# Padding written early, one wide product of U and x, wide idle products and a longer allowance for GpSimd in a scheduled recurrence with a two-layer MLP

## The chip, the cores and the metric

One NeuronCore of a Trainium2 chip runs the whole program. The time is that of one execution in microseconds (us), as the device reports it; lower is better. Five engines work side by side, each through its own instructions in order: PE multiplies matrices (its weight loads are listed as PEld), DVE, ACT and POOL (GpSimd) do elementwise work, SP issues transfers, and ACT issues a few.

## The reference

For each of 4 batches and 8 heads a recurrence runs over 768 steps with a state of 48x48, and its output, 768 rows of 384 numbers for each batch, goes through a mixing term of rank 32 over the sequence and a two-layer MLP:

```python
for t in range(S):
    cur = einsum('bhd,bhe->bhde', u * k[t], v[t])
    y[t] = einsum('bhd,bhde->bhe', r[t], state + cur)
    state = w[:, None] * state + einsum('bhd,bhe->bhde', k[t], v[t])
x = y                                    # (4, 768, 384)
h = x.transpose(0, 2, 1) @ U @ V         # U: 768x32, V: 32x768
u_ = x + h.transpose(0, 2, 1)
out = u_ + relu(u_ @ w_ch1) @ w_ch2      # 384 -> 1536 -> 384
```

The inputs r, k, v, w and u are 32-bit floats. U, V and the two weight matrices are 64-bit floats.

## The kernel before

**Tiling.** A batch is cut into 6 chunks of 128 rows. Within a chunk the recurrence is written as products: scores of r with k (`pab`, L751), which a mask turns into `am` (L885), the scores times v (`pav`, L787), the carried state times r (`pav`, L793), and the new state from the scaled k and v (`pab`, L766; then `S`, L913, and its decayed copy `SW`, L922 or L926). r and k come in row by row and are turned on PE (`ptr`, `ptk`, L712); the turned copies are scaled into `rT` and `kT` by DVE or ACT. The scaled k itself is `ks` (L662): 8 heads of 48 numbers, each padded to 64 with zeros that a GpSimd memset writes (L661). There are two `ks` buffers. The diagonal term is `dv` (L669, L671, L681). The result of chunk n is `x` (L892).

The work of chunk n stands on PE in two halves, called first(n) and second(n) here: each does half of the outputs of chunk n and half of the scores of chunk n + 1. second(n) begins only after one small copy named `seen` (L866) of the first half's result.

**Order.** No loop runs on the chip. Python records every step as an operation with its engine, an estimate of its duration, what it reads and writes, and a key that gives its rank. `Plan.schedule` then plays the operations through its own estimates and fixes the order on each engine; where an operation may run on several engines (`on_either`, `one_of`), the estimates choose one. So a changed estimate may move instructions anywhere. Engines still wait for data by semaphores. Where the plan expects PE to idle, `plan.wakes` puts in products of the identity with itself that nobody reads (`wake`); it does so from the first product until the last product of U and x of batch 0, and in a second stretch behind it.

**Front.** Batch 0 has nothing to run beside. Its six chunks of attention come first (about 11 to 49 us). Each chunk's x is multiplied with U into the bank `wk` (`c_gx`, shown as `wake<-x,Uf`), the sum becomes `Gs` (L947, L948), and products of `Gs` and V finish the turned input of the MLP (`pu`, split into `uTh` and `uTl`). Meanwhile the 64-bit weights arrive and are made into floats, split in two parts: per block of 128x384 a pick of the high byte (L518 on DVE or L522 on ACT), a scale on ACT (L534), two integer operations on DVE (L525, L528), a rounded copy on ACT (L548) and a difference (L549, DVE or POOL). U and V go the same way (`raw_u`, `raw_v`).

**Rest.** From the first `p` product on, PE works through the MLP of batch 0 with the attention of batch 1 put in between, and so on through the batches. Each unit of the MLP is 9 products of 128x384 for the first layer and 9 for the second; the next attention fills the gaps.

Of the kernel before, what the change touches and what calls it, by code (L numbers as in the profile page):

```python
# [46 lines left out]
class Plan:  # L47
# [98 lines left out]
    def schedule(self):  # L146
        free = dict.fromkeys(self.AFTER, 0.0)
        cands = {e: [] for e in free}
        waiting, blocked = {}, []
        lock, queues, tiled, flying = 0.0, 0.0, False, {}  # L150
        for o in self.ops:
            o.behind -= o.deps
            waiting[o] = len(o.deps) + len(o.behind)
            o.out = []
        for o in self.ops:
            for p in o.deps | o.behind:
                p.out.append(o)

        def admit(o):
            for b in o.allocs:  # L160
                ring = self.rings[b.tag]
                k = sum(1 for x in o.allocs[:o.allocs.index(b)] if x.tag == b.tag)
                if ring["next"] + k >= len(ring["order"]) or ring["order"][ring["next"] + k] is not b:
                    return False
                if sum(f is not None for f in ring["free"]) <= k:
                    return False
            o.early, o.ends = max((p.start for p in o.behind), default=0.0), [(p.end, p.eng) for p in o.deps]
            for b in o.allocs:
                ring = self.rings[b.tag]
                i = min((i for i, f in enumerate(ring["free"]) if f is not None), key=lambda i: ring["free"][i][0])  # L170
                o.ends.append(ring["free"][i])
                if ring["last"] is not None:
                    o.early = max(o.early, ring["last"].start)
                ring["free"][i] = None
                ring["next"] += 1
                ring["last"] = o
                b.slot = i
            for i, way in enumerate(o.ways):
                cands[way[0]].append((o, i, self.ready_on(o, way[0])))
            return True  # L180

        def offer(os):
            blocked.extend(os)
            again = True
            while again:
                again = False
                for o in sorted(blocked, key=lambda o: o.key):

                    if all(self.rings[b.tag]["last"] is None or self.rings[b.tag]["last"].end is not None
                           for b in o.allocs) and admit(o):  # L190
                        blocked.remove(o)
                        again = True
        for o in self.ops:
            o.end = None
        offer([o for o in self.ops if not waiting[o]])
        left = len(self.ops)
        while left:
            best = None
            for e, cs in cands.items():
                if not cs:  # L200
                    continue
                at = []
                for o, i, ready in cs:
                    t = max(ready, free[e])
                    if o.ways[i][3]:
                        t = max(t, lock - (130 if e == "DVE" else 0))
                    at.append((t, o, i))
                now = min(t for t, _, _ in at)
                for t, o, i in sorted((a for a in at if a[0] <= now + 1), key=lambda a: a[1].key):
                    done = t + o.ways[i][1]  # L210
                    if e == "DVE" and len(o.ways) > 1:
                        done += self.BACKLOG * sum(q.ways[k][1] - self.OVERLAP[e] for u, q, k in at if u <= t and q.key > o.key)
                    if any(j != i and self.queue(o, w, cands[w[0]], free[w[0]], lock) < done - 1
                           for j, w in enumerate(o.ways)):
                        continue
                    if best is None or t < best[0]:
                        best = (t, o, i)
                    break
            t, o, i = best
            e, ns, fn, lk = o.ways[i]  # L220
            for w in o.ways:
                cands[w[0]] = [c for c in cands[w[0]] if c[0] is not o]
            if e == "PE":
                for begin, end, filler in self.wakes:
                    if begin.end is None or end.end is not None:
                        continue

                    x = free[e]
                    while self.pe_end(x, begin.ways[0][1], 0, False) < t - 150:
                        self.woken.append((x, filler))  # L230
                        x = self.pe_end(x, begin.ways[0][1], 0.8)
                        tiled = False
                    t = max(t, x)
                if o.tiled != tiled:
                    t, tiled = t + self.MODE, o.tiled
                ns = self.pe_end(t, ns, 0.65 if tiled else 0.85) - t
            o.start, o.eng, o.fn = t, e, fn
            free[e] = t + ns - self.OVERLAP[e]
            o.end = t + ns
            if lk:  # L240
                lock = o.end
            if o.dma:
                ring = flying.setdefault(e, [])
                room = self.RING - o.rows
                issued = t + ns
                for end, rows in reversed(ring):
                    room -= rows
                    if room < 0:
                        issued = max(issued, end)
                        break  # L250
                free[e] = issued + self.ISSUE[e]
                queues = max(queues, issued if issued == t + ns else t + ns) + o.dma
                ring.append((queues, o.rows))
                o.end, o.eng = queues + self.LANDS + o.late, "DMA"
            left -= 1
            new = []
            for p in o.out:
                waiting[p] -= 1
                if not waiting[p]:
                    new.append(p)  # L260
            for b in o.bufs:
                b.left -= 1
                if not b.left and b.tag:
                    end = max((u[0].end + (self.DRAINS if u[0].eng == "PE" else 0), u[0].eng) for u in b.uses)
                    self.rings[b.tag]["free"][b.slot] = end
            offer(new)
        return max(o.end for o in self.ops)
# [8 lines left out]
def dve(n):  # L276
    return 130 + 1.09 * n
# [6 lines left out]
def pool(n):  # L284
    return 180 + 2.15 * n
# [3 lines left out]
def rwkv_moe(ctx: ExitStack, tc: tile.TileContext, r, k, v, w, u, U, V, w1, w2, out):  # L289
    nc = tc.nc  # L290
    B, H, S, D = r.shape
    C = 128
    NCH = S // C
# [47 lines left out]
    def whole(*args, **kw):  # L341

        opened.clear()
        return nc.tensor.matmul(*args, **kw)  # L344

    def pe(ns, fn, w_, r_, tiled=False, dk=0.0):
        return op("PE", ns, fn, w_, r_, tiled=tiled, dk=dk)
# [6 lines left out]

    def on_either(n, fn, w_, r_, dk=0.0, only=None):

        ways = [("POOL", pool(n), lambda: fn(nc.gpsimd), True), ("DVE", dve(n), lambda: fn(nc.vector), True)]
        return one_of(ways, w_, r_, only, dk)

    def one_of(ways, w_, r_, only=None, dk=0.0):  # L360
# [38 lines left out]
    wk = bank("mm", "wake")  # L399
    awake = []  # L400

    def waking(bank_):

        def fn():
            whole(bank_.t[:, :128], lhsT=ident_, rhs=ident_, start=bank_ not in awake, stop=True, skip_group_check=True)
            awake.append(bank_)
        return fn

# [248 lines left out]
    def a_ks(n):  # L657

        kt, kb = ks_[n]
        ks = kss[n] = wbuf([128, H, HP], F32, "ks", NK, f"ks_{n}")  # L660
        op("POOL", 250, lambda: nc.gpsimd.memset(ks.t[:, :, D:], 0.0), [(ks, "pad")], [])  # L661
        on_either(384, lambda e: e.tensor_mul(ks.t[:, :, :D], kt()[:, :, :D], by_head(tab.t)), [(ks, "d")], kb + [tab],  # L662
                  only="DVE" if front(n) else None)

# [269 lines left out]

    def c_gx(n):

        for i in range(3):
            o = pe(225, lambda i=i: whole(wk.t[:3 * R, 128 * (i + 1):128 * (i + 2)], lhsT=Uf.t[:, n].rearrange("p k r -> p (k r)"),
                                      rhs=xs[n].t[:, 128 * i:128 * (i + 1)], start=False, stop=n == NCH - 1,
                                      skip_group_check=True), [(wk, "g")], [Uf, xs[n]])  # L940
        return o

    def c_g0():
        def pt():
# [359 lines left out]
    for t, _, f in sorted(steps, key=lambda s: s[:2]):  # L1304
        plan.key = t
        f()
    plan.wakes = [(*ends, gx[-1], fill), (*again, refill)]
    with tc.manual_schedule(engines={mybir.EngineType.PE, mybir.EngineType.SP, mybir.EngineType.DVE,
                                     mybir.EngineType.Activation, mybir.EngineType.Pool}):
        plan.run()  # L1310
# [34 lines left out]
```

## Time and profile before

| what | value |
|---|---|
| median of 3 runs | 438.04 us (437.14 to 439.49) |
| the profiled execution | 439.95 us, span 437.9 us |
| PE busy | 419.4 us (96%) |
| DVE busy | 267.8 us (61%) |
| ACT busy | 142.9 us (33%) |
| POOL busy | 55.6 us (13%) |
| mean granted clock of PE | 0.984 |

The span is what the profile covers; 2.05 us of the profiled execution's own time lie outside it. A granted clock of 1.00 is 2.4 GHz, one of 0.50 is 1.2 GHz. A busy share over the whole span says little here, since the front has other limits than the rest.

### The profile page before, as it was taken

To read this page: it belongs to the slowest core of one execution; us is meant where nothing else is said; L and a number is where in the kernel's file an instruction comes from. 1 tells how busy PE (TensorE), PEld (TensorE's weight loads), DVE (VectorE), ACT (ScalarE), POOL (GpSimd) and SP (SyncE) were. 2 spreads that over 40 slices of the span, in tenths; PEclk is the share of its full clock that TensorE was granted. 3 is DMA by queue.
4 is the path that set the end of the run, shared out by engine and by line. 5 is a ranking of instruction groups with operands and counts; after the bars stand their busy time and mean duration, and the time that the engine had idled before them with its cause. 6 is when DMAs were issued, how large, how long until landed. Compare 5 with 4: busy or idle time off the path is not lost.

```text
span 437.9 us, 12193 instructions
## 1 busy us (share of the span) xinstructions
PE 419.4 (96%) x5125; PEld 399.8 (91%) x5125; DVE 267.8 (61%) x602; ACT 142.9 (33%) x399; POOL 55.6 (13%) x92
## 2 busy tenths in 40 slices
PE   8889999999999999999999999999999999999991
PEld 8678899889999999999999999999999999999991
DVE  6979699999887757767775456567522351122121
ACT  1679679934421213121112221222112131111110
POOL 2651151223110002011100001101100000000000
PEclk9989699999999999999999999999999999999998
DMA  9979999654466876744586653231100510001001
GB/s 145 162 162 340 335 199 222 103 84 83 81 88 139 148 146 117 136 87 76 105 168 102 96 147 56 48 64 30 55 2 1 98 65 1 0 0 55 1 0 61
DMA packets 178975, 43.93 MB, mean 100 GB/s; under 512 B 168993, under 2 KB 175650, under 8 KB 178914
## 3 DMA queue, kind: packets, MB, share of 16 engines
q1 hardware_dynamic: 174162, 42.20, 46.9%
q10 hardware_dynamic: 4752, 0.89, 1.5%
q8 instruction: 42, 0.69, 0.7%
q14 instruction: 19, 0.16, 0.1%
HBM read 36.57 MB, written 6.49 MB: 98 GB/s over the span
## 4 chain that ended last, share of the span: by engine, by line
PE 81%; DVE 8%; ACT 3%; DMA 3%; POOL 1%; issue 1%; SPq 0%; ACTq 0%; DVEq 0%; POOLq 0%
PE p L344 64%; PE pav L787 5%; PE pav L793 4%; PE pu L344 3%; DVE raw_w L528 2%; DVE raw_w L525 2%; PE pab L751 2%; DMA ld<-in_r_dram 1%; DMA ld<-in_v_dram 1%; PE pab L766 1%; PE wake L344 1%; DVE hl L1081 1%; PE pG L958 1%; ACT dv L681 1%; POOL dv L671 1%
## 5 line engine op out<-in xcount | busy, mean ns | idle before, releaser
L344 PE MATMUL p<-uTh,w1s 128*128 128x384 f32 x576 | 148.2, 338 | 0.0
L1081 DVE SCALAR_TENSOR_TENSOR hl<-p,hh 128x384 fp32r<-128x384 f32 x96 | 53.2, 554 | 119.3 <-ACT hh L1080 119.0
L344 PE MATMUL p<-w2s,hh 128*128 128x384 f32 x576 | 120.3, 340 | 0.6 <-ACT hh L1080 0.6
L1080 ACT ACTIVATE hh<-p 128x384 fp32r<-128x384 f32 x96 | 47.2, 491 | 210.3 <-PE p L344 208.7
L344 PEld LDWEIGHTS p<-uTh,w1s 128*128 128x128 f32 x576 | 102.9, 188 | 0.8
L344 PEld LDWEIGHTS p<-w2s,hh 128*128 128x128 f32 x576 | 99.8, 188 | 2.8 <-ACT hh L1080 0.9
L344 PE MATMUL p<-uTl,w1s 128*128 128x384 f32 x288 | 96.4, 335 | 0.0
L344 PE MATMUL p<-w2s,hl 128*128 128x384 f32 x288 | 65.8, 335 | 0.0
L344 PEld LDWEIGHTS p<-uTl,w1s 128*128 128x128 f32 x288 | 54.0, 188 | 0.0
L344 PEld LDWEIGHTS p<-w2s,hl 128*128 128x128 f32 x288 | 51.4, 188 | 0.0
L787 PE MATMUL pav<-vsw,am 64*64 64x48 f32 x384 | 33.0, 226 | 0.6 <-DVE am L885 0.5
L793 PE MATMUL pav<-S,rT 48*64 48x48 f32 x704 | 32.0, 222 | 0.9 <-issue 0.9
L787 PEld LDWEIGHTS pav<-vsw,am 64*64 64x64 f32 x384 | 26.7, 137 | 6.1 <-issue 4.1
L751 PE MATMUL pab<-rT,kT 48*64 48x64 f32 x768 | 31.2, 228 | 0.3 <-DVE rT L721 0.2
L793 PEld LDWEIGHTS pav<-S,rT 48*64 48x64 f32 x704 | 27.9, 139 | 1.0 <-issue 1.0
L751 PEld LDWEIGHTS pab<-rT,kT 48*64 48x64 f32 x768 | 25.1, 137 | 1.5 <-DVE rT L721 0.5
L787 PE MATMUL pav<-ldv,am 64*64 64x48 f32 x320 | 26.5, 222 | 0.0
L787 PEld LDWEIGHTS pav<-ldv,am 64*64 64x64 f32 x320 | 21.5, 134 | 4.7 <-issue 3.9
L885 DVE TENSOR_TENSOR am<-pab,mask 128x256 f32<-128x256 f32 x48 | 19.7, 417 | 6.8 <-PE pav L793 6.2
L661 POOL MEMSET ks<- 128x128 f32 x24 | 4.9, 205 | 133.2 <-PE pab L766 66.8
L766 PE MATMUL pab<-ldv,ks 64*48 64x48 f32 (+1 forms) x576 | 21.0, 212 | 0.0
L926 ACT ACTIVATE SW<-S,wm 112x48 f32<-112x48 f32 x48 | 12.2, 324 | 21.3 <-DVE S L913 20.0
(127 smaller groups left out, 515.5 us busy)
## 6 DMA issues: line engine op xcount, KB each, us to landing
raw_w<-in_moe_w_ch_dram SPq DMA_DIRECT2D x24, 384.0 KB, 7.4
out_dram<-x SPq DMA_DIRECT2D x24, 192.0 KB, 2.0
ldr<-in_r_dram SPq DMA_DIRECT2D x20, 192.0 KB, 3.3
ldk<-in_k_dram SPq DMA_DIRECT2D x20, 192.0 KB, 3.6
ldv<-in_v_dram SPq DMA_DIRECT2D x20, 192.0 KB, 3.6
bl<-in_r_dram SPq DMA_DIRECT2D x79, 48.0 KB, 2.6
bl<-in_k_dram SPq DMA_DIRECT2D x79, 48.0 KB, 2.5
vsw<-in_v_dram SPq DMA_DIRECT2D x42, 48.0 KB, 3.2
```

The costliest lines, as they stand in the source:

```text
L344: return nc.tensor.matmul(*args, **kw)
L525: nc.vector.scalar_tensor_tensor(word(0), word(1), -2 ** 31, word(0), ALU.bitwise_and, ALU.bitwise_or)
L528: nc.vector.scalar_tensor_tensor(word(0), word(1), 3, word(0), ALU.logical_shift_left, ALU.bitwise_or)
L661: op("POOL", 250, lambda: nc.gpsimd.memset(ks.t[:, :, D:], 0.0), [(ks, "pad")], [])
L751: return [lambda q=q, i=i: nc.tensor.matmul(pt.t[(i ^ j) * C2:(i ^ j) * C2 + C2, q * C2:(q + 1) * C2], lhsT=kT.t[rows, q, i * C2:(i + 1) * ...
L766: return nc.tensor.matmul(pt.t[j * HP:j * HP + m, SU + q * D:SU + (q + 1) * D], lhsT=ks.t[half, 2 * q + j, :m], rhs=vt()[half, 2 * q + j, ...
L787: return nc.tensor.matmul(to(q, j, i), lhsT=am[j].t[half, q, :], rhs=vsw[n].t[half, q, :] if j else vt()[half, 2 * q, :], start=(row == RO ...
L793: return nc.tensor.matmul(to(q, row, i), lhsT=rT.t[rows, q, i * C2:(i + 1) * C2], rhs=St[n, i].t[rows, q, :], start=False, stop=(row == RO ...
L885: on_dve(256, lambda e: e.tensor_tensor(am.t, abs_[n][j].t[:, :SU].rearrange("p (h t) -> p h t", h=NP), mask_.unsqueeze(1).broadcast_to([1 ...
L926: nc.scalar.activation(dec.t[:, q], new.t[:, q], AF.Copy, scale=wm.t[:, q])
L1080: on_act(384, lambda: nc.scalar.activation(hh.t, pt.t[:, :TB], AF.Relu), [hh], [pt])
L1081: on_dve(384, lambda e: e.scalar_tensor_tensor(hl.t, pt.t[:, :TB], 0.0, f32(hh.t), ALU.max, ALU.subtract), [hl], [pt, hh])
```

## The change

The new kernel has four edits, all in the tables and rules from which the order is made.

1. The memset of the padding of `ks` gets the key minus 20, so that it ranks ahead of nearly everything that is ready on GpSimd.
2. `c_gx` multiplies a chunk's x with U in one product of 384 columns in place of three of 128, with 655 ns as estimate in place of three times 225.
3. While the plan's clock stands below 8000 ns, idle time of PE is filled with products of 512 columns (estimate 870 ns) where one fits; they write a bank of the tag `av`. Narrow ones follow as before.
4. An operation that is given to GpSimd alone (`only="POOL"`: the products for `dv` of chunks 1 to 5 of batch 0) is estimated at 1.3 times its former duration.

```diff
-                for begin, end, filler in self.wakes:
+                for begin, end, filler, *more in self.wakes:
...
                     x = free[e]
+                    for long, ns_, until in more:
+                        while x + ns_ / self.clock(x) < min(t, until) - 150:
+                            self.woken.append((x, long))
+                            x = self.pe_end(x, ns_, 0.8)
...
-        ways = [("POOL", pool(n), lambda: fn(nc.gpsimd), True), ("DVE", dve(n), lambda: fn(nc.vector), True)]
+        ways = [("POOL", pool(n) * (1.3 if only else 1.0), lambda: fn(nc.gpsimd), True), ("DVE", dve(n), lambda: fn(nc.vector), True)]
...
-    def waking(bank_):
+    def waking(bank_, n=1):
...
-            whole(bank_.t[:, :128], lhsT=ident_, rhs=ident_, start=bank_ not in awake, stop=True, skip_group_check=True)
+            whole(bank_.t[:, :128 * n].rearrange("p (a c) -> p a c", a=n), lhsT=ident_,
+                  rhs=ident_.unsqueeze(1).broadcast_to([128, n, 128]), start=bank_ not in awake, stop=True,
+                  skip_group_check=True)
...
-        op("POOL", 250, lambda: nc.gpsimd.memset(ks.t[:, :, D:], 0.0), [(ks, "pad")], [])
+        op("POOL", 250, lambda: nc.gpsimd.memset(ks.t[:, :, D:], 0.0), [(ks, "pad")], [], dk=-20.0)
...
-        for i in range(3):
-            o = pe(225, lambda i=i: whole(wk.t[:3 * R, 128 * (i + 1):128 * (i + 2)], lhsT=Uf.t[:, n].rearrange("p k r -> p (k r)"),
-                                      rhs=xs[n].t[:, 128 * i:128 * (i + 1)], start=False, stop=n == NCH - 1,
-                                      skip_group_check=True), [(wk, "g")], [Uf, xs[n]])
-        return o
+        return pe(655, lambda: whole(wk.t[:3 * R, 128:], lhsT=Uf.t[:, n].rearrange("p k r -> p (k r)"), rhs=xs[n].t,
+                                     start=False, stop=n == NCH - 1, skip_group_check=True), [(wk, "g")], [Uf, xs[n]])
...
-    plan.wakes = [(*ends, gx[-1], fill), (*again, refill)]
+    plan.wakes = [(*ends, gx[-1], fill, (waking(bank("av", "wake0"), 4), 870, 8000)), (*again, refill)]
```

The order on the engines differs from the first filled wait on until well into the MLP of batch 0. Lines of the new kernel stand 3 to 6 higher (L661 becomes L667, L712 becomes L718, L721 becomes L727). Three places matter.

The first is PE behind second(1), where first(2) follows; ks_534 is the scaled k of chunk 4, and pav_573 the output of chunk 2. Before:

```order
L712 MATMUL ptk_511<-ident,ks_408 128x128 x4
L712 MATMUL ptr_529<-ident,ld_106 128x128 x4
L712 MATMUL ptk_549<-ident,ks_534 128x128 x4
L712 MATMUL ptr_565<-ident,ldr_111 128x128 x2
L787 MATMUL pav_573<-vsw_150,am_1_514 64x48
L751 MATMUL pab_0_575<-rT_557,kT_543 64x64
```

The same place in the new kernel, where the turn of the scaled k of chunk 4 (ks_542) stands behind first(2), and idle products stand ahead of it:

```order
L718 MATMUL ptr_474<-ident,ld_107 128x128 x2
L348 MATMUL wake<-ident 128x128 x5
L793 MATMUL pav_559<-vsw_150,am_1_552 64x48
L757 MATMUL pab_0_561<-rT_549,kT_475 64x64
...
L348 MATMUL wake<-ident 128x128
L718 MATMUL ptk_609<-ident,ks_542 128x128 x2
```

So the turn of k of chunk 4 no longer stands ahead of first(2), and the turn of r of chunk 3 has moved up behind second(1).

The second place is DVE around the x of chunk 2 (x_723 before, x_681 now) and the turned r of chunk 4 (rT_664, rT_698). Before:

```order
L721 TENSOR_TENSOR rT_664<-ptr_565,tabT 112x512
L677 TENSOR_REDUCE dg_672<-dv_568 128x8
L885 TENSOR_TENSOR am_1_678<-pab_1_630,mask 128x256
L913 TENSOR_TENSOR S_1_686<-pab_1_630,SW_1_662 112x192
L892 TENSOR_TENSOR x_723<-pav_573,dv_283 128x384
L662 TENSOR_TENSOR ks_682<-ldk_119,tab 128x8x48
```

In the new kernel:

```order
L683 TENSOR_REDUCE dg_659<-dv_554 128x8
L891 TENSOR_TENSOR am_1_665<-pab_1_621,mask 128x256
L919 TENSOR_TENSOR S_1_676<-pab_1_621,SW_1_615 112x192
L898 TENSOR_TENSOR x_681<-pav_559,dv_281 128x384
L524 TENSOR_SCALAR raw_u<-raw_u 128x192
L524 TENSOR_SCALAR raw_v_531<-raw_v_531 96x384
L727 TENSOR_TENSOR rT_698<-ptr_673,tabT 112x512
```

rT of chunk 4 stood ahead of x of chunk 2; now it stands behind it and behind two byte picks that ACT did before.

The third place is DVE ahead of the turned r of chunk 5. Before, it stands right behind the x of chunk 3 (x_853):

```order
L892 TENSOR_TENSOR x_853<-pav_688,dv_394 128x384
L721 TENSOR_TENSOR rT_862<-ptr_836,tabT 112x512
L518 TENSOR_SCALAR raw_w_1_0_675<-raw_w_1_0_675 128x384
L525 SCALAR_TENSOR_TENSOR raw_w_0_0_668<-raw_w_0_0_668 128x384
L525 SCALAR_TENSOR_TENSOR raw_w_1_0_675<-raw_w_1_0_675 128x384
```

In the new kernel:

```order
L898 TENSOR_TENSOR x_833<-pav_711,dv_379 128x384
L565 TENSOR_TENSOR V_803<-raw_v_552,V_803 32x384
L668 TENSOR_TENSOR ks_671<-ldk_119,tab 128x8x48
L531 SCALAR_TENSOR_TENSOR raw_w_0_0_653<-raw_w_0_0_653 128x384
L531 SCALAR_TENSOR_TENSOR raw_w_1_0_661<-raw_w_1_0_661 128x384
L534 SCALAR_TENSOR_TENSOR raw_w_0_0_653<-raw_w_0_0_653 128x384
L534 SCALAR_TENSOR_TENSOR raw_w_1_0_661<-raw_w_1_0_661 128x384
L531 SCALAR_TENSOR_TENSOR raw_w_2_0_669<-raw_w_2_0_669 128x384
L727 TENSOR_TENSOR rT_875<-ptr_860,tabT 112x512
```

Seven instructions now lie between them, among them the scaled k of chunk 5 (ks_671), which stood behind the x of chunk 2 before (ks_682, above).

## Rows read from the trace of the kernel before

**Rows 1.** Page, span in 40 slices: granted clock of PE in tenths.

```profile
PEclk9989699999999999999999999999999999999998
```

**Rows 2.** Stretches: us, busy of PE, PEld, DVE, ACT, POOL, clock, DMA, GB/s.

```profile
60.00:80.00 20.00, 19.38 (x112) 18.80 (x111) 19.70 (x37) 18.43 (x52) 5.56 (x5) 1.00 0.81 175
...
300.00:400.00 100.00, 100.00 (x885) 97.78 (x884) 34.83 (x71) 18.34 (x40) 2.54 (x3) 1.00 0.12 31
```

**Rows 3.** Chain that ended last, 49 to 53 us: start, us, what.

```profile
49.03 2.43 PE pu L344 x10
51.46 1.71 PE wake L344 x8
```

**Rows 4.** Stretches of the front, columns as in rows 2.

```profile
24.00:27.30 3.30, 1.31 (x12) 0.91 (x9) 2.41 (x6) 3.12 (x14) 2.46 (x4) 1.00 0.65 122
27.30:30.70 3.40, 3.40 (x95) 2.94 (x98) 1.37 (x5) 2.54 (x11) 2.26 (x3) 0.54 1.08 239
...
47.80:51.20 3.40, 3.40 (x40) 3.31 (x37) 2.47 (x6) 2.43 (x6) 0.00 (x0) 0.54 1.03 389
51.20:54.60 3.40, 3.40 (x18) 3.40 (x17) 1.59 (x3) 1.82 (x4) 0.82 (x1) 0.50 0.95 213
```

**Rows 5.** Waits of PE, whole span: total us, times, longest.

```profile
PE ptk L712 <- POOL ks L661: 2.0, 1, 2.0
PE ptk L712 <- DVE ks L662: 1.9, 2, 1.2
...
PE pav L793 <- issue: 0.9, 1, 0.9
PE p L344 <- ACT hh L1080: 0.6, 1, 0.6
```

**Rows 6.** Timeline, idle products and the table's turn: start, us, instruction.

```profile
1.67 3.79 PE L344 MATMUL wake<-ident 128*128 128x128 f32 x16 [1.67 <-POOL ident masks.py:199]
...
7.68 1.28 PE L344 MATMUL wake<-ident 128*128 128x128 f32 x10
8.98 0.60 PE L460 MATMUL pt_tab<-ident,tw 112*128 112x112 f32 x4
```

**Rows 7.** Timeline of DVE: the table that PE turns.

```profile
8.23 0.69 DVE L452 TENSOR_TENSOR tw<-tabT,wm 112x512 f32<-112x512 f32 x1
```

**Rows 8.** Timeline of PE: products of U and x; products of Gs and V.

```profile
39.32 0.90 PE L344 MATMUL wake<-x,Uf 128*96 128x128 f32 x6
...
59.41 0.69 PE L344 MATMUL p<-Gs,V 96*128 96x384 f32 x3
```

**Rows 9.** Timeline of DVE: scaled k alone, S of chunk 1, scaled k beside GpSimd, x of chunk 5.

```profile
15.16 0.54 DVE L662 TENSOR_TENSOR ks<-ld,tab 128x384 f32<-128x384 f32 x1
...
19.92 0.34 DVE L913 TENSOR_TENSOR S<-pab,SW 112x192 f32<-112x192 f32 x1
...
20.98 1.51 DVE L662 TENSOR_TENSOR ks<-ld,tab 128x384 f32<-128x384 f32 x1
...
49.07 0.56 DVE L892 TENSOR_TENSOR x<-pav,dv 128x384 f32<-128x384 f32 x1 [0.93 <-PE pav L793]
```

**Rows 10.** Timeline of PE: starts of first(1), first(2), first(3), first(4), then Gs with V, first `p`.

```profile
20.65 0.31 PE L787 MATMUL pav<-vsw,am 64*64 64x48 f32 x2
...
27.25 0.31 PE L787 MATMUL pav<-vsw,am 64*64 64x48 f32 x2
...
32.11 0.25 PE L787 MATMUL pav<-vsw,am 64*64 64x48 f32 x1
...
40.15 0.25 PE L787 MATMUL pav<-vsw,am 64*64 64x48 f32 x1
...
54.91 1.30 PE L344 MATMUL pu<-V,Gs 96*128 96x384 f32 x6
...
56.20 0.60 PE L344 MATMUL p<-uTh,w1s 128*128 128x384 f32 x2
```

**Rows 11.** Chain that ended last: two conversion steps on DVE.

```profile
73.99 0.94 DVE raw_w L528 x2
```

## Prediction

> **What bounds the kernel now.** I read the page's slices first: the granted clock of PE stays at nine tenths or more, that is at full speed, except in a few early slices and the last one [rows 1]. From the stretches the reader is to see that there are two stages. Between 300 and 400 us PE is busy for all 100 us while DVE has 34.83 [rows 2]: there PE alone is the limit, and the diff takes nothing from PE's work. So whatever the change is worth must show as an earlier start of the first MLP product, which stands at 56.20 us [rows 10], or as waits of PE soon behind it. Between 60 and 80 us DVE is busy 19.70 of 20 us and PE 19.38 [rows 2]; the weights are still being converted there.
>
> In the front PE's waits are few but dear. The list of waits names 2.0 us for the GpSimd padding of the scaled k, 1.9 for scaled k on DVE, 0.9 with no releaser seen ("issue") and 0.6 for ACT's `hh`, which lies behind 56 us [rows 5]. The first is followed by something dearer than itself: in 24.0 to 27.3 us PE was busy for 1.31 us only, and in the next 3.4 us its granted clock was 0.54, that is mostly the lower of its two levels [rows 4]. The same happens from 47.8 to 54.6 us, at 0.54 and 0.50 [rows 4], and there PE is on the chain that ended last: ten `pu` products take 2.43 us and eight `wake` products 1.71 [rows 3]. PE was busy through these 6.8 us, so the clock alone cost it about half of them, 3.2 us (0.46 of 3.4 and 0.50 of 3.4).
>
> **The edits themselves.**
>
> *Wide idle products.* Eight narrow ones at the start become one of 512 columns and four of 128: 8 times 128 columns in both. Five before the table's turn become one of 512 and one of 128, again the same columns. They took 3.79 and 1.28 us [rows 6]. The turn `pt_tab` starts at 8.98 [rows 6] behind `tw` on DVE, which ends at 8.92 [rows 7], so DVE sets it. I take 0. That cover holds as long as the wide one is not so late that it ends behind 8.92; at the lower clock it could take up to 512/128 x 0.47 (3.79 over 8 products) = 1.9 us in place of 4 x 0.26, a loss of 0.9 at most. A gain is excluded, since DVE comes last.
>
> *One product of U and x.* Three narrow ones take 0.90 us at full clock [rows 8]. No row has the wide one. Its rows of 384 columns cost at least what `p<-Gs,V` costs, 0.69/3 = 0.23 each, and each of these products is listed as two, so 0.46 is the lower end and 0.90 the upper. I take 0.65, as both ends come from products with other weights or types. Six times it saves 0.25, but only the last of the six stands between the last x and `Gs`: 0.25 us of gain, 0 to 0.44.
>
> *Early padding.* The memset itself is not on the path any more: GpSimd still writes the padding for chunk 4 behind both `dv` products, as there is a free `ks` buffer only after second(1). But PE's order moved that turn behind first(2), so the 2.0 us wait [rows 5] goes from there.
>
> *Longer allowance for GpSimd.* It adds no work; it only changes choices.
>
> A product of scaled k took DVE 0.54 us alone and 1.51 beside a GpSimd product [rows 9]. The Trainium skill (GPSIMD Engine Reference, Specifications) says that GpSimd shares its SBUF interfaces with VectorE and that they contend when VectorE reads two SBUF inputs. By that rule scaled k of chunk 3, which falls beside a `dv` product again, takes the 1.51, and first(1) below comes at 23.4; without it, at 22.4. The sum changes by nothing, because x of chunk 5 hangs on later conversions.
>
> **What the new order does to the front.** I followed the new order by hand with durations of the old trace. A half of attention on PE takes 1.25 us at full clock; `S`, `am` and `x` take DVE 1.06 together (19.92 to 20.98, [rows 9]); a conversion step 0.47 (0.94 over 2, [rows 11]); turned r 0.6.
>
> - first(1) was at 20.65 [rows 10]. DVE now turns r of chunk 2 behind scaled k of chunk 3: second(0) ends at about 19.8, then S, am, x 1.06, SW 0.3, scaled k 0.5 to 1.5, r 0.6: 22.4 to 23.4. I take 23.0, 2.4 us later.
> - first(2) was at 27.25 [rows 10], held by the padding. Now: 23.0, two halves and the r turns of chunk 3, 25.9, then am, S, x and turned r on DVE 1.7: about 27.8. So 0.55 later, but PE fills the wait with five idle products, the clock should stay up, and second(2) ends at 30.8 in place of 31.5.
> - first(3) was at 32.11 [rows 10]. Turned r of chunk 4 now stands behind x of chunk 2 and two byte picks: 31.0 + 1.06 + 0.7 + 0.6 = 33.4, 1.3 later.
> - first(4) was at 40.15 [rows 10]. Between x of chunk 3 (38.6) and turned r of chunk 5 stand seven steps, 7 x 0.47 = 3.3, then 0.6: 42.6, 2.5 later.
> - x of chunk 5 was at 49.07 [rows 9]. In the new order DVE is full up to it; it comes at about 50.0, 1.0 later. The old order lost the 0.9 issue wait here.
> - From x of chunk 5 to the first MLP product it took 7.1 us (49.07 to 56.20), nearly all at half clock. At full clock: x 0.5, last product of U and x 0.65, ACT free after 0.4, `Gs` 0.45 and 0.6, then 1.3 as from 54.91 to 56.20 [rows 10]: 4.0. The first `p` is at 54.0, 2.2 earlier.
>
> Behind it, all three parts of the fourth unit now stand ahead of the second layer of the third, so the 0.6 us wait for `hh` [rows 5] should go. The edit to the product of U and x is inside the 4.0.
>
> **The sum.** 439.95 of the profiled execution - 2.2 - 0.6 = 437.15. The profiled execution lies 1.9 above the median of its three runs, and the clock may have been up for longer in those, which the change could not give back. So from 438.04 the sum by the trace would be 435.2, if the runs lost as much to the clock, and 438 if they lost nothing. I forecast **437.0 us**, faster by 0.2%, which a measurement of this kernel can hardly tell from no change; I count 0.5%, 2.2 us, as the least that it can.
>
> **Rivals.**
>
> 1. *The clock falls again ahead of the last products.* For it: the half clock began behind a stretch of mostly small attention products, with PE 0.9 idle, and the new order has the same mixture there and about as much waiting. Against it: fewer narrow products and more idle ones. Then the 3.2 us come back: first `p` at 56.8 or later, minus 0.6 behind it: 439.95 + 0.6 - 0.6 = about 440 in the profile's terms, 438.5 to 440 as a run. No change.
> 2. *DVE is what the front hangs on, and its idle time goes.* DVE idled 0.9, 2.0, 0.9 and 1.8 us in the four stretches of [rows 4], 5.6 in all. Were all of it regained for the conversions, the first `p` and what follows would be 5.6 earlier: 434.3. For it: DVE is full from 60 to 80 us. Against: my walk finds new waits of DVE for ACT and GpSimd in the early chunks.
> 3. *Conversions ahead of attention cost more than the clock gives.* Turned r of chunks 4 and 5 now stands behind steps that wait for a transfer of V and for ACT, on an engine that works in order; `seen` on ACT too stands behind such steps, and PE waits for both. If ACT's steps come late, DVE's seven steps take 0.9 apiece in place of 0.47, 3.0 us more at first(4), and as much in the conversions before x of chunk 5. It decides from x of chunk 5 at about 53 us on (3.1 behind my value); at 55 the time is 442. Slower.
>
> **How the numbers follow.** The forecast has 0.38, rival 1 0.20, rival 2 0.28, rival 3 0.14. The forecast's own range is 435.9 to 438.3 (first(1) by [rows 9], the product by its bounds, the first clock stretch). Faster by over 0.5% (under 435.85) comes from rival 2 and the lower edge of the forecast: 0.33. Slower by over 0.5% (over 440.2) is rival 3 and the upper edge of rival 1: 0.15. The rest, 0.52, is within 0.5%. The range that leaves out two in ten cuts into rival 2 below and leaves out rival 3 above: 433.8 to 440.2.
>
> **What would show it.** Right: no wait of PE for the padding; first(1), first(3) and first(4) later than before while the first `p` is near 54; a granted clock of 1.00 from 27 to 31 and from 48 to 54 us; no 0.6 us wait for `hh`. Wrong: a clock of 0.5 in 48 to 54 us (rival 1), the first `p` before 52 (rival 2) or x of chunk 5 after 53 (rival 3), or a loss behind 60 us, where I assume that the shift is kept to the end.

## Result and the profile after: slower by 0.4%

| | median us (range, runs) | profiled execution | first `p` in it |
|---|---|---|---|
| before | 437.92 (436.15 to 440.76, 20) | 439.95 | 56.20 [rows 10] |
| after | 439.91 (438.17 to 441.79, 20) | 439.93 | 55.87 |

The ratio is 1.0041, interval 1.0023 to 1.0058; the forecast was 437.0. The two profiled executions take the same time. The old one was 2.0 us above its median, the new one stands at its own, so these two profiles alone can't show the loss.

The waits of PE after (total, times, longest), which answer to [rows 5]:

```profile
PE pab L757 <- ACT raw_v L540: 1.7, 1, 1.7
...
PE pav L793 <- DVE am L891: 1.6, 2, 1.1
PE pab L757 <- DVE rT L727: 1.5, 3, 0.8
PE ptk L718 <- DVE ks L668: 1.2, 2, 1.0
...
PE p L348 <- DVE w2s L555: 0.3, 1, 0.3
PE pav L793 <- issue: 0.3, 1, 0.3
```

The wait for the padding and the one for `hh` are gone, as forecast; the first one listed is new. The stretches after answer to [rows 4], the last two of them to [rows 2]:

```profile
24.00:27.30 3.30, 3.06 (x99) 2.79 (x91) 2.73 (x7) 1.39 (x7) 2.53 (x4) 1.00 0.79 150
27.30:30.70 3.40, 3.40 (x89) 3.08 (x83) 0.96 (x3) 2.42 (x11) 2.29 (x4) 1.00 0.96 225
30.70:34.00 3.30, 1.03 (x42) 0.79 (x43) 3.30 (x10) 2.96 (x10) 0.65 (x2) 1.00 0.56 100
34.00:38.00 4.00, 4.00 (x106) 3.24 (x98) 3.87 (x10) 3.95 (x13) 0.86 (x3) 0.54 0.90 320
38.00:41.70 3.70, 3.70 (x8) 1.68 (x7) 3.66 (x9) 2.83 (x6) 0.56 (x2) 0.57 1.02 389
...
51.20:54.60 3.40, 3.40 (x35) 3.05 (x31) 2.51 (x5) 2.77 (x7) 0.46 (x1) 1.00 0.90 208
60.00:80.00 20.00, 19.40 (x112) 18.72 (x110) 20.00 (x39) 18.81 (x53) 6.05 (x5) 1.00 0.79 181
...
300.00:400.00 100.00, 100.00 (x885) 97.79 (x884) 35.37 (x72) 18.33 (x40) 2.53 (x3) 1.00 0.11 31
```

The half clock has moved: none at 27 to 31 and 51 to 55 us, but 0.54 and 0.57 from 34 to 41.7, behind 3.3 us in which PE was busy for 1.03. The four wide products of U and x lie in it, and are on the chain that ended last, as `pu` was in [rows 3]:

```profile
37.27 4.69 PE wake L348 x8
```

The timeline of DVE after shows what is late ahead of it:

```profile
30.43 0.55 DVE L683 TENSOR_REDUCE dg<-dv 128x8 f32<-128x384 f32 x1 [2.16 <-POOL dv L677]
```

And the timeline of PE after has the starts that answer to [rows 10]: first(1), first(3), first(4), first `p`.

```profile
21.70 0.25 PE L793 MATMUL pav<-vsw,am 64*64 64x48 f32 x1
...
33.43 0.24 PE L757 MATMUL pab<-rT,kT 48*64 48x64 f32 x1 [1.75 <-ACT raw_v L540]
...
44.33 0.25 PE L793 MATMUL pav<-vsw,am 64*64 64x48 f32 x1
...
55.87 0.60 PE L348 MATMUL p<-uTh,w1s 128*128 128x384 f32 x2
```

DVE waits for GpSimd's `dv` of chunk 5 and has `am`, `S` and x of chunk 2 and turned r of chunk 4 queued behind it, so first(3) starts at 33.43. The profile puts that wait down to ACT's `raw_v`, which a `pab` product doesn't read; of what it does read, turned k was done at 32.7 and turned r, on DVE, at 33.3. first(4) comes 4.2 us later than in [rows 10]. x of chunk 5 is at 51.52.

### The profile page after: what moved, and what is told of

It reads as the page before. It is cut to its first block, busy times and chain, and to the rows that moved or that the text cites. A ratio compares the mean times of both kernels' runs of the same rounds, so it can differ in the third digit from the quotient of the medians.

```text
span 437.8 us, 12161 instructions
## 1 busy us (share of the span) xinstructions
PE 420.2 (96%) x5105; PEld 396.8 (91%) x5105; DVE 264.9 (61%) x601; ACT 143.8 (33%) x402; POOL 57.4 (13%) x93
## 4 chain that ended last, share of the span: by engine, by line
PE 82%; DVE 10%; ACT 2%; DMA 2%; POOL 1%; issue 1%; ACTq 0%
PE p L348 64%; PE pav L793 5%; PE pav L799 4%; PE pu L348 3%; DVE raw_w L534 2%; PE pab L757 2%; DVE raw_w L531 2%; PE wake L348 2%; PE pab L772 1%; DMA vsw<-in_v_dram 1%; DVE hl L1084 1%; PE pG L961 1%; ACT dv L687 1%; DMA ld<-in_k_dram 1%; DVE uTl L1016 1%
## 5 line engine op out<-in xcount | busy, mean ns | idle before, releaser
L793 PE MATMUL pav<-vsw,am 64*64 64x48 f32 x384 | 33.3, 226 | 1.9 <-DVE am L891 1.6
L667 POOL MEMSET ks<- 128x128 f32 x24 | 5.1, 211 | 133.5 <-PE pab L772 63.5
L932 ACT ACTIVATE SW<-S,wm 112x48 f32<-112x48 f32 x52 | 13.1, 323 | 21.0 <-DVE S L919 19.7
```

What stands on the lines that cost most here:

```text
L793: return nc.tensor.matmul(to(q, j, i), lhsT=am[j].t[half, q, :], rhs=vsw[n].t[half, q, :] if j else vt()[half, 2 * q, :], start=(row == RO ...
L932: nc.scalar.activation(dec.t[:, q], new.t[:, q], AF.Copy, scale=wm.t[:, q])
```

## The experiments

Medians with range, the ratio to the kernel before as measured beside it, and from the profiled execution its time, the start of x of chunk 5 and of the first `p` (us):

| run | median | ratio, interval | profile: time, x5, first `p` |
|---|---|---|---|
| a1 | 442.58 (441.78 to 444.03) | 1.0101, 1.0063 to 1.0139 | 444.03, 53.70, 59.59 |
| a2 | 438.12 (436.72 to 439.49) | 1.0003, 0.9980 to 1.0026 | 439.49, 49.56, 53.93 |
| a3 | 437.70 (436.18 to 441.30) | 1.0018, 0.9987 to 1.0048 | 436.79, 47.39, 51.77 |
| a4 | 437.19 (436.56 to 439.05) | 0.9986, 0.9960 to 1.0012 | 437.09, 48.03, 52.38 |
| b1 | 440.54 (438.37 to 442.98) | 1.0047, 1.0010 to 1.0085 | 442.98, 53.26, 59.15 |
| b2 | 442.90 (441.08 to 445.62) | 1.0120, 1.0068 to 1.0173 | 442.04, 50.72, 56.66 |
| b3 | 442.90 (441.73 to 443.84) | 1.0103, 1.0070 to 1.0136 | 443.20, 53.81, 59.64 |
| b4 | 441.14 (439.88 to 443.38) | 1.0079, 1.0045 to 1.0113 | 441.92, 51.95, 57.54 |
| c1 | 442.07 (440.43 to 442.52) | 1.0094, 1.0057 to 1.0131 | 440.43, 50.21, 54.56 |
| c2 | 439.79 (438.03 to 441.73) | 1.0035, 1.0012 to 1.0058 | 440.51, 50.52, 54.88 |
| c3 | 439.75 (438.54 to 443.34) | 1.0050, 1.0023 to 1.0076 | 438.95, 51.33, 55.67 |
| d1 | 440.41 (439.46 to 442.04) | 1.0059, 1.0038 to 1.0080 | 442.04, 50.38, 54.73 |
| d2 | 437.50 (436.52 to 439.66) | 0.9998, 0.9981 to 1.0015 | 436.56, 47.92, 52.29 |
| d3 | 440.81 (439.04 to 443.60) | 1.0071, 1.0042 to 1.0099 | 441.44, 50.77, 56.64 |
| d4 | 439.46 (438.83 to 440.36) | 1.0030, 1.0009 to 1.0052 | 438.83, 50.13, 54.48 |
| e1 | 439.35 (438.14 to 443.38) | 1.0047, 1.0021 to 1.0073 | 442.22, 53.12, 58.28 |
| e2 | 439.04 (437.64 to 443.87) | 1.0040, 1.0011 to 1.0070 | 437.83, 49.66, 54.03 |
| e4 | 439.65 (438.56 to 440.69) | 1.0046, 1.0025 to 1.0067 | 440.55, 51.70, 57.21 |

**Which edit.** a1 has the allowance alone, a2 the three others, a3 the wide idle products alone, a4 none.

```diff
# a1, the only edit
-        ways = [("POOL", pool(n), lambda: fn(nc.gpsimd), True), ...
+        ways = [("POOL", pool(n) * (1.3 if only else 1.0), lambda: fn(nc.gpsimd), True), ...
```

> The kernel before with the longer allowance for GpSimd alone. It gives the order of the whole change on DVE, ACT, GpSimd and SP row for row; only the shapes of the idle products and of the products of U and x stay narrow. If the new order costs the 2.0 us (order theory): 439.5 to 440.5 us. If the wide products cost it (product theory): 437.5 to 438.3 us.

> The whole change without the longer allowance: padding key, wide product of U and x, wide idle products. Order theory: 437.0 to 438.5 us, since the new order is gone (another, smaller move of order comes with the wide product's estimate). Product theory: 439.5 to 440.5 us.

> The kernel before with two wide idle products in place of eight narrow ones, nothing else moved. Order theory: no change, 437.4 to 438.4 us, first turn of the table at 8.9 to 9.0 us as before. Product theory: slower, 438.5 us or more.

> The kernel before unchanged, for a second profile. Both theories: about 437.9 us. If the half clock of the first profile (27.3 to 30.7 and 47.8 to 54.6 us) hangs on chance, it stands elsewhere or is shorter here, and the span is some 2 us shorter than 437.9; if it belongs to the order, it is at the same places.

The loss comes with the allowance: alone it costs 4.85 us (442.58 against 437.73), and the three other edits without it stay at the time of the kernel before. a4 brought something else: the same program as before without the half clock. Its stretches, which answer to [rows 4]:

```profile
24.00:27.30 3.30, 1.37 (x33) 1.23 (x36) 2.85 (x5) 3.29 (x15) 1.37 (x4) 1.00 0.73 138
27.30:30.70 3.40, 3.08 (x131) 2.62 (x127) 2.58 (x8) 2.51 (x11) 2.77 (x5) 1.00 1.03 232
...
51.20:54.60 3.40, 3.31 (x20) 2.99 (x20) 3.37 (x6) 3.40 (x10) 1.41 (x2) 1.00 0.68 173
```

And its first `p` on the timeline of PE:

```profile
52.38 0.60 PE L344 MATMUL p<-uTh,w1s 128*128 128x384 f32 x2
```

PE was busy for 1.37 of the first 3.3 us here and 1.31 in [rows 4], and the clock fell behind the one and not behind the other. So the first `p` of the old order is at 52.4, 3.8 us ahead of [rows 10], when the clock stays up (51.77 in a3, whose clock was 1.00 from 24 to 57 us).

**One wait removed, one filled, one wide product less.**

b3 undoes edit 2 and b4 edit 3, as in the diff of the change. The other two in the order of an engine, shortened:

```diff
# b1, DVE
-dg (chunk 5)
 am_1, S_1, x (chunk 2)
 picks of raw_u, raw_v
 rT (chunk 4)
+dg (chunk 5)
# b2, PE ahead of first(3)
-MATMUL wake<-ident 128x128 x4
+MATMUL wake<-ident 128x128 x13
```

> The changed kernel with one DVE instruction moved: the diagonal sum dg of chunk 5, which waits 2.16 us for GpSimd's dv of that chunk (28.27 to 30.43 us), stands behind the turned r of chunk 4 in place of ahead of am, S and x of chunk 2. Nothing else moves but two pairs of dv products on ACT that need it. Wait theory (this wait is where the new order loses): turned r of chunk 4 ends near 31.2 us in place of 33.3, first(3) starts near 31.4 in place of 33.4, PE idles under 0.6 us there in place of 2.3, the clock then stays at 1.00 from 34 to 42 us, the first p product comes at 53 or before in place of 55.9, and the time falls by 2 to 3 us, to 437 to 438. Rival (conversion theory: x of chunk 5 hangs on DVE's and ACT's conversions, whatever the early chunks do): first(3) comes earlier, but x of chunk 5 stays near 51.5 us, and the time within 0.7 us of the changed kernel's 439.9.

> The changed kernel with nine more idle products of 128 columns on PE ahead of first(3), where it idles from 30.8 to 33.4 us (9 x 0.26 = 2.35 us). DVE's order and its wait for dv stay. Clock theory (PE's idling ahead of first(3) is what lets the granted clock fall, and the half clock is what costs): first(3) stays at 33.4, the clock is 1.00 from 34 to 42 us, the eight gx rows on the chain take about 2.6 us in place of 4.69, the first p comes 1.5 to 3 us earlier, the time is 437 to 438.4. Wait theory (the late start is what costs, PE has slack behind it): the clock may stay up, but the first p stays within 0.7 us of 55.9 and the time within 0.7 us of 439.9.

> The changed kernel with three products of U and x of 128 columns again in place of one of 384; the order of everything else is the same. The allowance alone took 442.6, all four edits 439.9, so one of the two wide products gives 2.7 us back in this order. If it is the wide product of U and x: about 442.5 here, with more time in gx ahead of first(4) and the first p at 58 to 60. If it is the wide idle product at the start, or neither (two runs of the same order that fell differently by the clock): within 0.7 us of 439.9.

> The changed kernel with narrow idle products alone at the start; everything else is the same. If the wide idle product gives the 2.7 us back: about 442.5 here. If it is the wide product of U and x or neither: within 0.7 us of 439.9. By the forecast made before the result the idle product was worth nothing either way, so 439.9.

b1 refutes the wait theory in its simple form. The wait for `dv` was gone, x of chunk 2 came at 29.69 in place of 31.49, and DVE then waited for the next thing in its order, the transfer of V, as its timeline shows:

```profile
30.16 0.28 DVE L530 TENSOR_SCALAR raw_u<-raw_u 128x192 int32<-128x192 uint8 x1
32.34 0.36 DVE L530 TENSOR_SCALAR raw_v<-raw_v 96x384 int32<-96x384 uint8 x1 [1.90 <-DMA raw_v<-in_moe_V_dram]
32.62 0.68 DVE L733 TENSOR_TENSOR rT<-ptr,tabT 112x512 f32<-112x512 f32 x1
```

b2 speaks against the clock theory without settling it: the clock stayed at 1.00 from 30 to 48 us, x of chunk 5 came only 0.8 us earlier than in the changed kernel, and then the clock fell to 0.50 at 51 to 54 instead; the median was 3 us worse. b3 is as dear as a1: with narrow products of U and x the new order takes 442.9. b4 fits neither of its two forecasts: at 441.14 it is 1.2 us above the changed kernel, and the two intervals overlap, so that what the wide idle products are worth in the new order is not shown.

**The turned r of chunks 4 and 5 put back.** c1 moves the turn of chunk 5, c2 that of chunk 4 ahead of both of its waits, c3 does both.

```diff
# c1, DVE
 x (chunk 2)
+ks (chunk 5)
...
 x (chunk 3)
+rT (chunk 5)
 V
-ks (chunk 5)
 five conversion steps
-rT (chunk 5)
# c1, PE (turned k moves on ACT with it)
+ptk x4, ptr x4 (chunk 5)
 wake<-x,Uf 96x384 x4
-ptk x4, ptr x4 (chunk 5)
# c2, DVE
-dg (chunk 5)
 am_1, S_1, x (chunk 2)
+rT (chunk 4)
+dg (chunk 5)
 picks of raw_u, raw_v
-rT (chunk 4)
```

> The changed kernel with the turn of chunk 5 put back to where the old order has it: scaled k of chunk 5 behind x of chunk 2 on DVE, its turn and that of r ahead of the four wide products of U and x on PE, turned r right behind x of chunk 3 on DVE, turned k on ACT likewise. Turn theory (the third place of the change costs it: x of chunk 3 comes at 38.0 us in both orders, x of chunk 4 at 43.3 in the old one without half clock and at 47.8 in the new one, as turned r of chunk 5 comes 4.5 us later): first(4) moves from 44.3 to about 41, x of chunk 5 from 51.5 to about 48.5, the first p from 55.9 to about 53, time 437. Clock theory: PE has 37.2 to 44.3 us full anyway, most of it at half clock (four wide products take 4.4 us there), so first(4) stays near 44 and the time near 439.9.

> The changed kernel with DVE's turned r of chunk 4 ahead of both things that held it one after the other: the diagonal sum that waits for GpSimd, and the byte pick of V that waits for its transfer (1.90 us, to 32.3 us, in the run that moved the sum alone). Wait theory: turned r of chunk 4 ends near 30.9 us in place of 33.3, first(3) starts near 31 in place of 33.4, PE's 2.3 us of idling there go, the clock stays at 1.00 from 34 to 42 us, and the first p comes 1.5 to 2.5 us earlier: 437.5 to 438.5. Turn theory: first(3) comes earlier, but turned r of chunk 5 still comes behind x of chunk 3 and seven steps, and x of chunk 5 stays within 0.7 us of 51.5: 439.9.

> Both of the other two edits together; allowance, wide products and everything else stay as in the changed kernel. If these moved instructions are all that the allowance costs, the first p comes at 52 to 53 us, PE's clock stays at 1.00 from 24 to 56 us, and the time is that of the kernel before or better: 436 to 437.9. If the loss lies elsewhere (the conversions ahead of S, am and x of chunk 3; the waits between 80 and 93 us), 439 or more.

None came back to 438; c1 is 2.2 us dearer than the changed kernel. In c1 and c3 second(4) waited for its `seen` on ACT, in c2 second(3). The timeline of PE of c2 (line numbers stand up to 18 higher in these kernels):

```profile
35.15 0.34 PE L810 MATMUL pav<-ld,am 64*64 64x48 f32 x1 [2.16 <-ACT seen L889]
```

And that of c3:

```profile
46.20 0.25 PE L810 MATMUL pav<-ldv,am 64*64 64x48 f32 x1 [1.54 <-ACT seen L889]
```

**Both orders at full clock.** Idle products fill PE's waits: 20 more in the new order (d1), 16 in the old one (d2), 21 in c3's (d3); d4 is the changed kernel again.

```diff
# d2, ahead of four places in PE's order (d1, d3 likewise)
+MATMUL wake<-ident 128x128 x4    # turn of k of chunk 2
+MATMUL wake<-ident 128x128 x7    # turn of k of chunk 4
+MATMUL wake<-ident 128x128 x2    # second(3)
+MATMUL wake<-ident 128x128 x3    # second(4)
```

> The changed kernel with twenty more idle products on PE, put ahead of the five places where it waited in the profiles of this order (16.5, 21, 31 to 33.4, 39.5 and 46 us). Clock theory (the new order loses by half clock, not by its waits): clock 1.00 from 20 to 56 us, first p at 53 to 54, time 437 to 438.5, no more than 0.7 us from d2. Order theory (the late turned r of chunks 4 and 5 cost it whatever the clock): the clock may be up, first p still at 55 or later, time 439.5 or more, 1.5 us or more above d2.

> The kernel before with sixteen more idle products on PE, ahead of the four places where it waits (15.3, 26, 32.8 and 45.7 us). Clock theory: the half clock that its first profile showed at 27 to 31 and 48 to 55 us cannot come, first p at 52 to 52.5 as in the profile without half clock, time 436.5 to 437.5, that is 0.5 to 1 us better than before's median. Order theory: its order had no cost by the clock in most executions, so 437.5 to 438.2, no difference.

> The changed kernel with both moves of c3 and twenty-one more idle products ahead of its waits. Clock theory: with the clock up and turned r of chunks 4 and 5 early, first p at 52 to 53, time 436.5 to 437.5, as good as d2. If the loss is in seen on ACT (1.4 and 1.5 us of PE's waits in c3) or in the conversions, first p at 54 or later and 438.5 or more.

> The changed kernel as it is. Clock by chance: the half clock stands in other stretches than 17 to 20 and 34 to 42 us, and the time of the profiled execution moves with it by a us or more. Clock by the order: the same stretches again. The median is near 439.9 by both.

This decides between clock and order: at full clock in the front the new order is still 2.9 us behind the old one by the medians of d1 and d2. d2 and d1 both ran at 1.00 from 20 us to the first `p`, d4 from 24 us on, and the first `p` is at 52.29 in the old order, 54.73 and 54.48 in the new one. x of chunk 3 came at 37.39, 37.40 and 38.15, so the loss lies behind it. The stretches from x of chunk 3 to x of chunk 4 and on to x of chunk 5, columns as in [rows 4], of d2:

```profile
37.39:42.77 5.38, 5.25 (x134) 4.68 (x135) 5.32 (x14) 5.38 (x14) 0.64 (x2) 1.00 1.03 404
42.77:47.92 5.15, 4.38 (x81) 3.82 (x81) 3.02 (x8) 3.10 (x8) 0.64 (x1) 1.00 1.03 398
```

and of d4:

```profile
38.15:46.44 8.29, 7.28 (x144) 5.66 (x142) 8.25 (x19) 8.23 (x22) 0.95 (x4) 1.00 1.03 402
46.44:50.13 3.69, 3.37 (x69) 2.46 (x68) 2.90 (x8) 3.64 (x10) 1.04 (x1) 1.00 1.03 395
```

The third busy column is DVE. It is all but full up to x of chunk 4 in both, with 14 instructions in the old order and 19 in the new. By the written order, 12 conversion steps of U, V and the weights stand between x of chunk 3 and of chunk 5 before and 17 now (20 and 26 ahead of x of chunk 5 in all), and scaled k of chunk 5 besides. DVE works 11.15 us in place of 8.34, 2.8 more, and idles 0.8 in place of 2.2, 1.4 less: 1.45 us longer (11.98 against 10.53), and x of chunk 3 0.76 later make the 2.2 at x of chunk 5. In d1, where x of chunk 3 is not late, the same stretch takes 12.98. Behind x of chunk 5 the old order needs 4.37 us to the first `p` and the new one 4.35, and both need 384.3 us from there to the end (436.56 - 52.29, 438.83 - 54.48). d1 lost another 3 us behind its first `p` (442.04 - 54.73 = 387.3); its clock was 0.91 from 80 to 100 us. In d3 the idle products didn't hold the clock: it was 0.61 from x of chunk 4 to x of chunk 5 (45.96 to 50.77 us), so d3 says little about the two moves.

DVE is not alone in this. ACT, the fourth busy column, is as full: 5.38 of 5.38 and 3.10 of 5.15 us in d2, 8.23 of 8.29 and 3.64 of 3.69 in d4, which is 3.4 us more work. In d4 the chain that ended last runs ahead of first(4) through ACT, where turned k of chunk 5 stands behind conversion steps:

```profile
39.61 0.43 ACT raw_w L528
40.04 0.46 ACT raw_w L540
...
40.97 1.15 ACT kT L733 x4
```

In c1, c3 and d3, where turned k stands ahead of them, the chain goes from ACT's conversion steps to those of DVE that read them, and from there to `S` and `am` of chunk 5; in c3:

```profile
41.91 0.44 ACT raw_w L552
42.38 0.56 DVE raw_w L542
...
46.34 0.27 DVE S L937
```

**The rest of the chain.** e1 adds to c3 what stood behind conversions in chunk 4, e4 the same for chunk 3. e2 makes turned r of chunk 5 late in the old order; in it the four conversion steps that it was put behind also ran ahead of the scaling on ACT that they read, so they waited for nothing and worked on unscaled numbers.

```diff
# e1, ACT (seen of chunk 5 likewise; e4: seen of chunk 3 too)
+seen (chunk 4)
 five conversion steps
-seen (chunk 4)
# e1, DVE (e4: the same for chunk 3)
 rT (chunk 5), V, four conversion steps
+S, am_0 (chunk 5)
 two conversion steps
+am_1 (chunk 5), x (chunk 4)
 three w1s
-S, am_0 (chunk 5)
 two conversion steps
-am_1 (chunk 5), x (chunk 4)
# e2, DVE of the kernel before
 x (chunk 3)
-rT (chunk 5)
 pick and three conversion steps
+rT (chunk 5)
```

> The changed kernel with both moves of c3, and behind them the rest of the chain of chunk 4: seen of chunks 4 and 5 ahead of five conversion steps on ACT each, S and am of chunk 5 and x of chunk 4 ahead of five steps on DVE. Chain theory (the whole stretch of chunk 4 stands behind conversions in the new order, and one instruction put back only meets the next one): first(4) near 40.5, x of chunk 4 near 43.5 in place of 46.4, x of chunk 5 near 48.5 in place of 50.1, the first p at 52.5 to 53.2, time 437.0 to 438.2. Rival (total of conversions ahead of the first p sets it, whatever the order): x of chunk 5 earlier, but p products then wait for w1s and w2s, time 439.3 to 440.

> The kernel before with one instruction moved: DVE's turned r of chunk 5, right behind x of chunk 3 there, stands behind the four conversion steps that followed it (1.9 us). Chain theory: first(4) starts 1.9 us later, x of chunk 5 and the first p 1.0 to 1.9 us later (the old order has 0.8 us of PE and 1.6 us of DVE idling behind it that may take some), time 438.7 to 439.8. Rival (the late turn of chunk 5 is hidden by that idling): time within 0.5 us of the kernel before.

> The changed kernel with all moves of e1, and for chunk 3 the same: seen ahead of five entries on ACT (three of them conversions of V), S and am of the first half ahead of three conversion steps on DVE, S, am and x of the second half ahead of three. Now no step of chunks 2 to 5 stands behind a conversion that it was not behind in the old order. Chain theory: no wait of PE over 0.8 us between 28 and 48 us, x of chunk 3 at 36 to 37 us, x of chunk 5 near 48, first p near 52.5, time 437 to 438.2. If the conversions' total sets it: x of chunk 5 early, but waits of p products for w1s and w2s and DVE full, time 439 or more.

e2 went as the chain theory had it: turned r at 40.03, 2.2 us later than in d2, x of chunk 5 at 49.66, 1.7 later, the median 1.2 us up. Late turned r alone costs in the old order, by the median; its profile doesn't give the size, as the clock was 0.78 from x of chunk 3 to x of chunk 4 in it. e1 and e4 did not: their time is that of the changed kernel. They moved conversions from ahead of x of chunk 4 to between it and x of chunk 5, so that 26 steps still stand ahead of the latter. DVE was full between the two (idle 0.00 by the timeline), and x of chunk 5 came at 53.12 and 51.70, in both with stretches of half clock on the way. So moving `seen`, `S`, `am` and x of chunk 4 ahead of some of those steps didn't help while the steps stayed ahead of x of chunk 5. e4 also speaks for ACT: at a clock of 1.00 it needed 8.30 us from x of chunk 3 to x of chunk 4, as d4 did (8.29), although DVE had 16 instructions there in place of 19 and idled for about a microsecond; ACT was busy for 8.24 us.

## Why the prediction was wrong

**The failed step** is the first term of the sum, 439.95 - 2.2: "From x of chunk 5 to the first MLP product it took 7.1 us (49.07 to 56.20), nearly all at half clock. At full clock [...] The first `p` is at 54.0, 2.2 earlier." The walk of the new order was good: x of chunk 5 forecast at 50.0 and the first `p` at 54.0, measured at 50.13 and 54.48 in d4. What it was set against was wrong. The 56.20 was one execution of the old order; others have 51.77, 52.38 and, with its waits filled, 52.29. The old order doesn't bring that half clock each time, so the change couldn't give it back. In place of 2.2 us gained the runs show 2.2 lost at full clock, and 2.0 between the medians. The prediction saw the doubt ("the clock may have been up for longer in those") but counted it as less gain, not as a loss. Its own figures had the loss in them: without the 3.2 us that it put on the clock the old first `p` stands at 53.0, a microsecond ahead of the 54.0 of the new order. The other microsecond is x of chunk 5: the 49.07 that the walk was set against holds the half clock at 27.3 to 30.7 us too, and in a4 and d2 it is at 48.03 and 47.92.

**The early starts.** first(1) came at 21.70 (forecast 23.0) and first(3) at 33.43 (33.4). The second is right by accident: second(2) ended near 29 and not at 30.8, and the wait for `dv`, which the walk lacked, took the difference. The scaled k of chunk 3, for which the walk left 0.5 to 1.5 us, took 0.55 beside a GpSimd product that took 1.44 in place of 1.00; in [rows 9] it was the one to pay. first(4), forecast at 42.6, was at 44.33 with the half clock and 42.81 in d4.

**The wait for `hh`, 0.6 us.** It is gone from the list, but nothing came of it: from the first `p` to the end it is 383.75 us before (439.95 - 56.20) and 384.06 after.

**The wide product of U and x, 0.25 us.** Nothing, the lower end of its bounds. On the timeline of PE the three narrow ones of the last chunk in d2 take as long at full clock,

```profile
49.02 0.82 PE L354 MATMUL wake<-x,Uf 128*96 128x128 f32 x6
```

as the wide one of d4:

```profile
51.23 0.81 PE L348 MATMUL wake<-x,Uf 128*96 128x384 f32 x2
```

What I didn't foresee is that in the new order the narrow form takes 3 us more (b3). Both profiles of the new order with narrow products (a1, b3) show half clock twice; here the stretches of b3:

```profile
33.00:39.00 6.00, 5.50 (x133) 5.12 (x134) 5.16 (x13) 4.94 (x14) 1.08 (x3) 0.50 0.97 349
51.00:57.00 6.00, 6.00 (x53) 5.63 (x52) 2.68 (x5) 2.83 (x7) 2.02 (x2) 0.52 0.93 236
```

With wide ones d4 shows neither stretch and the changed kernel only the first, but b4, which has them too, shows both. Why stays open.

**Idle products and padding, 0**: right without the allowance (a2, a3); with it b4 leaves it open.

**The rivals.** Rival 3, given 0.14, has the sign, and the place that the runs point to: conversions ahead of attention cost more. Its reason, DVE's steps waiting for ACT, is not what d4 shows: DVE idled for 0.04 us up to x of chunk 4, so the steps were more and not slower. The chains of c1, c3 and d3 do show DVE's steps hanging on ACT's. Its mark, x of chunk 5 behind 53 us, was taken from the wrong base; 50.1 was enough. Rival 1 saw the clock fall again, but in another place, and d1, with the clock up, shows that this is not the loss. Rival 2 is refuted: DVE's idle time did shrink from 2.2 to 0.8 us, and more work ahead of x of chunk 5 took more than that.

a4 and the profile before are one program, with a granted clock of 1.00 in the one and 0.54 in the other at 27.3 to 30.7 us. The Trainium skill (TensorE: Matmul & The Clock Gate, Part 1) says of the warm-up at the start that it differs from run to run of the same kernel. These two traces don't show that at the start, where the first idle products take 3.79 us in both; they show a difference of this kind in the later stretches. Thought of at [rows 4], it would have been a reason to look at a second execution before the 2.2 us were counted.

**Open.** That the order which comes with the allowance is the loss is shown. That the six more conversion steps on DVE ahead of x of chunk 5 (five of them behind x of chunk 3) are what costs is argued, from the busy time and from the count: all kernels with 26 steps ahead have medians of 439.35 to 442.90, those with 19 or 20 and turned r in its place 437.19 to 438.12. But every kernel with 26 has the allowance and none of the others has, so the count goes along with all else that the allowance moves, ACT's conversions first of all. To take the steps out to behind x of chunk 5, on DVE or on ACT, was not tried. No kernel here beats the one before; d2 and a3 equal it.

## What to carry to other kernels

A profile is one execution: before a stretch of half clock is booked as something that a change can win back, look whether a second execution of the same kernel has it. In a kernel whose order comes from estimates, count how many instructions of background work the new order puts ahead of the last step of the critical chain on each full engine; that count went with the sign here, while each single wait, once removed, only uncovered the next. A longer estimate for one engine is not a local edit.

## What the runs showed of the hardware

One program can run at about half clock from 27.3 to 30.7 and from 47.8 to 54.6 us in one execution and at 1.00 there in another, with much the same waits: PE was busy for 1.31 of 3.3 us ahead of the fall in [rows 4], and for 1.37 of 3.3 in a4 and 1.27 in a3, where none came. With idle products in the gaps the clock was 1.00 from 20 us to the first `p` in d1 and d2, but in d3 it fell to 0.50 at 47.8 to 51.2 us, in b2 to 0.50 at 51 to 54, and in d1 it was 0.91 from 80 to 100; no kernel became faster by it.
